# Attention and MLP in one kernel: the first two sets' q and k in two parts, scrap products ahead of the scores, new instruction orders, short MLP stretches as four column tiles

## The chip, the cores and the metric

The kernel runs on one core of one Trainium2 chip. The metric is the device time of one execution in microseconds (us), here the median of three. The profile is one execution recorded by the hardware; its span runs from the first to the last instruction. TensorE (PE) multiplies, VectorE (DVE), ScalarE (ACT) and GpSimd (POOL) do the rest, and SP issues stores. POOL issues nearly all loads[...].

## The reference

```python
B, H, S, Nb, D = 8, 8, 576, 16, 64
k_all = concatenate([beacon_k, k], axis=2)
v_all = concatenate([beacon_v, v], axis=2)
scores = q @ k_all.T / sqrt(D)               # causal over k; every query sees the 16 beacons
a = softmax(scores)
attn = a @ v_all
x = attn.transpose(0, 2, 1, 3).reshape(B * S, H * D)     # 4608 x 512
h = x @ w_in                                  # 512 x 2048
out = (h * sigmoid(1.702 * h)) @ w_out        # 2048 x 512
```

## The kernel before

**Sets.** A set is one batch and four of its eight heads; there are 16 sets. The four heads lie on four groups of 32 partitions. A set's q and k are loaded by POOL (L349) into `qn` and `kn`: each partition takes 18 rows of 64 values. VectorE turns them (`e_turn`, L405) into `qT` and `kT`, with 32 of the 64 head dimensions on partitions and the other two halves side by side; the 16 beacon rows go through `bkf` and `bkn` into the head of `kT`.

**Scores and values.** `e_qk` (L434) computes scores of keys by queries in chunks of up to 512 columns for each of the four heads, as four row tiles of the array (32 rows each) at once. There is one score buffer `s` of four PSUM banks, so chunk i+1 waits until ScalarE has taken the exponential of chunk i (`e_exp`, L445). VectorE (first two sets) or POOL masks the diagonal blocks (L459, L466). `e_av` (L521) multiplies by the values, or by ones for the sums (x = 2), as four column tiles of the array (32 columns each), one head a tile. VectorE makes reciprocals of the sums (`e_z1`, `e_z2`) and scales the values into `xT` (`e_norm`, L556). The first four sets ("early") have their queries cut at `HF` = 288 into half 0 and half 1, and their chunks are cut so that the halves come one after the other; the first two sets' halves 0 come before everything else. Later sets are cut at 224.

**MLP.** Tokens are in groups: 0 and 1 of 256 tokens, then of 512. `e_m1` (L580) computes x @ w_in for a piece of a group, ScalarE (and for groups 0 and 1 VectorE) applies the gate, `e_m2` (L625) multiplies by w_out for groups 0 and 1; from group 2 to 9 a scheme of seven half-size products is used (`e_prod`, L694), with sums on VectorE (L645) and joins (`e_join`, L710). All these use the whole array. The values, m1, m2 and the products share a ring of four PSUM banks `u0` to `u3`; a bank is free again when its closer (gate, norm, evacuation or join) is done.

**Order.** Operations are numbered in the order in which the code creates them. `ORDER` (L16) lists for each engine the numbers in the order in which it executes them; POOL's loads are in POOL's list (Q holds their transfers). `Plan.run` (L146) only merges these lists into one by a model of times and emits the instructions; each engine then runs its own list strictly in order and waits on semaphores. At most eight loads are in flight (`LANES`). By name, TensorE's list begins qk0, qk1, qk2, then value passes of half 0 of sets 0 and 1 (av1.2.0, av0.2.0, av1.0.0, av0.0.0, av1.1.0, av0.1.0), qk3, qk4, m1.0.2, m1.0.0, qk5, m1.0.6, m1.0.4; here av s.x.half is set, x and half, and m1.g.n is group and column block.

Of the kernel before, what the change touches and what calls it, by code (L numbers as in the profile page):

```python
# [8 lines left out]
F32 = mybir.dt.float32  # L9
# [8 lines left out]
        76, 100, 106, 138, 115, 141, 118, 143, 120, 108, 111, 155, 152, 129, 161, 158, 122, 131, 164, 167, 134, 127,  # L18
        170, 173, 176, 145, 125, 148, 150, 177, 182, 188, 191, 227, 194, 197, 232, 183, 203, 234, 200, 178, 237,
        179, 206, 258, 241, 209, 184, 263, 185, 212, 265, 213, 248, 246, 268, 214, 215, 401, 251, 253, 272, 218,  # L20
        404, 275, 244, 279, 219, 220, 407, 282, 284, 277, 221, 414, 320, 296, 304, 290, 302, 292, 300, 298, 312,
        308, 294, 318, 314, 310, 306, 316, 426, 435, 423, 343, 338, 339, 340, 433, 431, 438, 344, 345, 359, 349,
        341, 464, 346, 350, 351, 352, 354, 574, 355, 429, 360, 361, 577, 356, 362, 357, 372, 365, 583, 474, 477,
        373, 366, 374, 367, 605, 480, 484, 375, 482, 607, 368, 506, 502, 488, 492, 610, 490, 486, 498, 504, 500,
        508, 514, 510, 516, 494, 496, 512, 534, 593, 596, 535, 536, 539, 540, 550, 541, 542, 537, 742, 545, 546,
        547, 548, 603, 745, 551, 552, 553, 599, 601, 619, 622, 748, 555, 556, 557, 558, 561, 755, 625, 627, 629,
        562, 563, 776, 568, 564, 569, 570, 571, 779, 764, 767, 659, 637, 641, 657, 649, 651, 647, 661, 635, 631,
        653, 805, 772, 770, 774, 643, 655, 633, 639, 645, 679, 680, 815, 818, 700, 681, 682, 684, 701, 915, 690,
        685, 686, 691, 692, 702, 918, 687, 693, 695, 703, 696, 924, 821, 823, 697, 698, 706, 946, 825, 707, 713,
        708, 709, 948, 934, 937, 714, 715, 716, 827, 951, 944, 940, 942, 853, 831, 833, 855, 857, 851, 843, 835,  # L30
        837, 847, 839, 845, 829, 849, 841, 1083, 960, 963, 875, 876, 880, 877, 878, 881, 882, 1086, 968, 966, 970,
        883, 1089, 902, 909, 903, 886, 891, 1096, 887, 888, 889, 892, 893, 1117, 904, 894, 905, 896, 897, 1120, 898,
        899, 910, 911, 1105, 1108, 1146, 912, 976, 994, 996, 972, 978, 1000, 992, 982, 974, 998, 990, 984, 988, 980,
        1002, 986, 1256, 1156, 1113, 1111, 1115, 1159, 1025, 1020, 1026, 1021, 1259, 1022, 1027, 1031, 1023, 1028,
        1265, 1164, 1162, 1166, 1041, 1042, 1287, 1036, 1047, 1032, 1048, 1033, 1037, 1038, 1034, 1039, 1289, 1054,
        1055, 1049, 1056, 1043, 1044, 1050, 1292, 1057, 1198, 1172, 1168, 1178, 1184, 1180, 1194, 1170, 1174, 1176,
        1275, 1278, 1182, 1186, 1196, 1188, 1190, 1281, 1301, 1285, 1283, 1304, 1216, 1217, 1221, 1192, 1222, 1227,
        1218, 1223, 1228, 1219, 1224, 1232, 1229, 1233, 1230, 1307, 1311, 1309, 1237, 1327, 1333, 1238, 1243, 1234,
        1244, 1235, 1323, 1239, 1245, 1250, 1251, 1341, 1240, 1246, 1252, 1253, 1337, 1405, 1315, 1331, 1343, 1411,
        1335, 1321, 1403, 1431, 1313, 1325, 1407, 1419, 1317, 1423, 1425, 1319, 1339, 1421, 1409, 1329, 1361, 1413,  # L40
        1366, 1382, 1429, 1362, 1363, 1401, 1367, 1364, 1427, 1368, 1383, 1372, 1369, 1373, 1374, 1375, 1388, 1377,
        1389, 1378, 1390, 1395, 1379, 1384, 1380, 1385, 1391, 1396, 1415, 1397, 1398, 1470, 1454, 1417, 1455, 1449,
        1471, 1450, 1451, 1476, 1452, 1456, 1477, 1457, 1478, 1460, 1461, 1462, 1463, 1465, 1466, 1467, 1468, 1472,
        1479, 1473, 1483, 1484, 1485, 1486,
    ],
    "ACT": [
        1, 3, 77, 79, 103, 101, 107, 109, 112, 153, 156, 130, 159, 162, 132, 165, 168, 135, 171, 174, 189, 192, 228,
        195, 198, 233, 235, 201, 204, 238, 180, 207, 259, 210, 264, 186, 266, 269, 216, 402, 405, 408, 222, 417,
        415, 297, 291, 303, 305, 301, 299, 293, 309, 321, 295, 319, 313, 315, 311, 307, 317, 436, 439, 342, 465,
        468, 575, 578, 584, 587, 606, 608, 503, 507, 489, 491, 493, 487, 499, 505, 509, 515, 517, 495, 501, 511,  # L50
        497, 513, 611, 538, 743, 746, 749, 756, 758, 777, 780, 660, 642, 638, 652, 658, 648, 650, 636, 632, 662,
        654, 806, 644, 634, 656, 640, 646, 809, 916, 683, 919, 928, 925, 947, 949, 952, 828, 832, 854, 856, 852,
        858, 834, 838, 844, 840, 836, 846, 830, 848, 850, 842, 1084, 879, 1087, 1090, 1099, 1097, 1118, 1121, 1147,
        1150, 977, 995, 979, 997, 993, 973, 975, 983, 991, 999, 989, 1001, 981, 1003, 985, 987, 1257, 1260, 1024,
        1269, 1266, 1288, 1290, 1293, 1199, 1179, 1173, 1181, 1185, 1195, 1171, 1169, 1175, 1177, 1183, 1187, 1197,
        1189, 1191, 1193, 1220, 1328, 1334, 1324, 1342, 1316, 1332, 1344, 1406, 1412, 1338, 1336, 1404, 1432, 1314,
        1408, 1420, 1318, 1424, 1326, 1426, 1320, 1340, 1422, 1410, 1330, 1322, 1414, 1430, 1402, 1365, 1428, 1416,
        1418, 1453,
    ],
    "DVE": [  # L60
        73, 74, 75, 97, 98, 99, 80, 81, 82, 78, 105, 87, 104, 102, 139, 116, 117, 121, 119, 140, 144, 142, 157, 154,
        123, 163, 160, 124, 224, 169, 128, 166, 172, 175, 146, 147, 126, 149, 151, 225, 226, 398, 190, 193, 196,
        199, 255, 256, 257, 202, 205, 286, 242, 411, 287, 211, 208, 243, 399, 249, 247, 400, 250, 412, 254, 252,
        273, 245, 274, 280, 276, 413, 281, 285, 283, 278, 289, 461, 288, 462, 419, 580, 420, 463, 326, 327, 328,
        421, 322, 92, 323, 324, 422, 427, 428, 424, 425, 325, 330, 334, 329, 335, 432, 336, 331, 434, 337, 332, 333,
        470, 347, 582, 353, 471, 581, 472, 430, 473, 358, 363, 475, 476, 478, 479, 481, 485, 739, 483, 369, 376,
        370, 589, 752, 740, 590, 615, 518, 753, 921, 519, 754, 526, 591, 527, 520, 528, 592, 529, 521, 741, 522,
        597, 523, 594, 530, 595, 598, 531, 802, 532, 524, 533, 616, 543, 525, 604, 549, 617, 618, 554, 600, 620,
        602, 623, 624, 621, 559, 760, 628, 761, 762, 626, 630, 565, 763, 566, 768, 572, 765, 811, 812, 766, 803,
# [47 lines left out]
class Plan:  # L117

    LAT = {"PE": 230, "ACT": 178, "DVE": 212, "POOL": 110, "Q": 1400, "SP": 0}

    def __init__(self, ring):
        self.ops = []
# [71 lines left out]
def kernel(  # L196
# [19 lines left out]
    P = 128  # L216
# [903 lines left out]
```

The softmax here doesn't subtract the row's maximum and nothing guards it: scores larger than these inputs give would overflow.

## Time and profile before

| what | value |
|---|---|
| median of 3 runs | 329.98 us (329.78 to 332.08) |
| span of the profiled execution (the page gives no other time for it) | 328.1 us |
| TensorE busy | 309.3 us, 4288 matmuls |
| first matmul | 8.38 us |
| VectorE, ScalarE, POOL busy | 235.9, 202.0, 114.0 us |
| turning k (128x576), one instruction | 1257 ns |
| first load (k of set 0): issued, landed | 1.30, 5.60 us |
| a w_in load of 256 KB, next landing after the last | about 1.26 us |
| transfers | 28.8 MB; engines nearly full until 57 us |

The times of runs are device times; the span is that of one execution, so a sum of steps is made against the span. In lines of the timeline the first number is the start, the second the length of a group of like instructions up to the end of the last; a matmul's end is modelled and overlaps the next one's start, so distances are taken from start to start. "32*128" is the part of the array in use, rows by columns.

### The profile page before, as it was taken

How to read it: one execution, taken by the hardware profiler on the slowest of the kernel's cores; microseconds unless marked ns; L12 is line 12 of the kernel's file. 1: busy time of each engine (PE TensorE's matmuls, PEld its weight loads, DVE VectorE, ACT ScalarE, POOL GpSimd, SP SyncE). 2: the span in 40 equal slices, each digit the busy share in tenths (PEclk: the TensorE clock that was granted, in tenths of full speed). 3: DMA queues.
4: the chain of work that ended last, by engine and by line, in shares of the span. 5: the costliest groups of instructions: out<-in, count | busy, mean ns of one | idle time of the engine just before them, and what ended most of it. 6: DMA issues, size and time to landing. Idle time of an engine off the chain costs nothing.

```text
span 328.1 us, 9811 instructions
## 1 busy us (share of the span) xinstructions
PE 309.3 (94%) x4288; PEld 210.0 (64%) x4288; DVE 235.9 (72%) x478; ACT 202.0 (62%) x236; POOL 114.0 (35%) x178
## 2 busy tenths in 40 slices
PE   0489999999999999999999999999999999999995
PEld 0367665544775467745878878547764776447884
DVE  3657788777987989977998798958557843006674
ACT  1567597687767686679767686868477212674010
POOL 8765487190319312951078019400042000000000
PEclk9999999999999999999999999999999999999999
DMA  7999999194424921693029809600120012000122
GB/s 126 161 202 209 203 187 181 34 99 103 113 67 72 186 50 34 70 191 57 2 45 177 133 2 122 157 0 2 37 96 2 2 34 78 18 0 2 65 98 97
DMA packets 58219, 28.81 MB, mean 88 GB/s; under 512 B 41280, under 2 KB 53568, under 8 KB 58176
## 3 DMA queue, kind: packets, MB, share of 16 engines
q0 software_dynamic: 47552, 18.49, 47.8%
q1 hardware_dynamic: 10560, 9.69, 9.1%
q8 instruction: 33, 0.54, 0.7%
q14 instruction: 10, 0.08, 0.1%
q10 hardware_dynamic: 64, 0.01, 0.0%
HBM read 37.22 MB, written 9.44 MB: 142 GB/s over the span
## 4 chain that ended last, share of the span: by engine, by line
PE 89%; ACT 4%; DVE 3%; DMA 2%; issue 1%; POOL 0%; DVEq 0%; ACTq 0%; POOLq 0%
PE u L580 36%; PE u L694 30%; PE s L434 9%; PE u L521 9%; PE u L625 4%; ACT E L445 3%; DMA qn<-in_q_dram 2%; DVE qT L405 1%; DVE sA L645 1%; DVE xT L556 1%; DVE rz L544 0%; DVE zt L533 0%; ACT L601 0%; DVE osb L710 0%; DVE rc L540 0%
## 5 line engine op out<-in xcount | busy, mean ns | idle before, releaser
L580 PE MATMUL u<-xT,w 128*128 128x512 f16 (+1 forms) x704 | 130.4, 340 | 0.5 <-ACT g L601 0.5
L445 ACT ACTIVATE E<-s 128x2048 f16<-128x2048 f32 (+5 forms) x66 | 98.9, 1515 | 46.0 <-PE s L434 45.6
L601 ACT ACTIVATE g<-u 128x512 f16<-128x512 f32 x128 | 70.5, 598 | 53.8 <-PE u L580 53.4
L580 PEld LDWEIGHTS <-w 128*128 128x128 f16 x704 | 67.8, 98 | 53.9 <-issue 1.5
L466 POOL TENSOR_SCALAR_AFFINE_SELECT E<-E 128x512 f16<-128x512 f16 (+3 forms) x78 | 49.3, 663 | 113.4 <-ACT E L445 81.6
L710 DVE SCALAR_TENSOR_TENSOR osb<-u,osb 128x512 f32<-128x512 f32 x56 | 37.2, 682 | 24.7 <-PE u L694 22.4
L694 PEld LDWEIGHTS <-g 128*128 128x128 f16 x512 | 48.4, 98 | 9.3 <-issue 0.2
L694 PE MATMUL u<-w,g 128*128 128x256 f16 x384 | 50.6, 273 | 0.0
L434 PE MATMUL s<-qT,kT 32*128 32x32 f16 (+20 forms) x1376 | 35.4, 232 | 14.4 <-DVE qT L405 8.4
L434 PEld LDWEIGHTS <-kT 32*128 32x128 f16 x1376 | 25.8, 94 | 30.6 <-issue 15.0
L694 PEld LDWEIGHTS <-sA 128*128 128x128 f16 x384 | 36.3, 98 | 5.3 <-issue 0.3
L694 PE MATMUL u<-tB,sA 128*128 128x256 f16 x256 | 35.0, 273 | 0.1
L645 DVE TENSOR_TENSOR sA<-g 128x512 f16<-128x512 f16 x32 | 12.9, 415 | 26.2 <-ACT g L601 26.2
L556 DVE TENSOR_TENSOR xT<-u,rz 128x352 f16<-128x352 f32 (+2 forms) x52 | 25.6, 517 | 6.9 <-PE u L521 6.7
L365 POOL DMA_DIRECT2D vb<-in_v_dram x32 | 27.4, 874 | 2.3 <-DMA kn<-in_k_dram 1.5
L521 PE MATMUL u<-E,vb 128*32 128x352 f16 (+8 forms) x928 | 28.0, 267 | 0.0
L484 DVE TENSOR_TENSOR zs<-zs,E 128x1344 f16<-128x1344 f16 (+2 forms) x36 | 22.7, 633 | 5.3 <-POOL E L466 4.4
L521 PEld LDWEIGHTS <-vb 128*32 128x32 f16 (+1 forms) x928 | 20.2, 99 | 5.9 <-issue 1.7
L405 DVE STREAM_TRANSPOSE kT<-kn 128x576 f32<-128x576 f32 x16 | 20.1, 1258 | 2.4 <-DMA kn<-in_k_dram 1.6
L405 DVE STREAM_TRANSPOSE qT<-qn 128x576 f32<-128x576 f32 x16 | 19.8, 1239 | 0.1
L533 DVE STREAM_TRANSPOSE zt<-u 128x224 f32<-128x224 f32 (+2 forms) x32 | 14.9, 471 | 6.6 <-PE u L521 6.5
L484 DVE TENSOR_TENSOR zs<-E 128x1856 f16<-128x1856 f16 x12 | 15.8, 1319 | 3.3 <-POOL E L466 3.3
(44 smaller groups left out, 237.7 us busy)
## 6 DMA issues: line engine op xcount, KB each, us to landing
out_dram<-osb SPq DMA_DIRECT2D x36, 256.0 KB, 2.5
kn<-in_k_dram POOLq DMA_DIRECT2D x16, 288.0 KB, 6.7
qn<-in_q_dram POOLq DMA_DIRECT2D x16, 288.0 KB, 6.6
vb<-in_v_dram POOLq DMA_DIRECT2D x24, 128.0 KB, 6.6
w<-in_moe_w_in_dram POOLq DMA_DIRECT2D x8, 256.0 KB, 9.9
w<-in_moe_w_out_dram POOLq DMA_DIRECT2D x4, 512.0 KB, 14.2
vb<-in_v_dram POOLq DMA_DIRECT2D x8, 112.0 KB, 5.0
vb<-in_v_dram POOLq DMA_DIRECT2D x8, 80.0 KB, 7.9
```

Of the source, the lines that this page charges most:

```text
L365: nc.gpsimd.dma_start(out=t[0 : hi - lo, j, h0:h1, :], in_=v[b, h0:h1, lo:hi, :].rearrange("h n d -> n h d"),)
L405: nc.vector.transpose(out=f32(dst.rearrange("p n e -> p (n e)")).rearrange("p (r t) -> p t r", t=TR), in_=f32(src[:, :]).rearrange("p (t c ...
L434: nc.tensor.matmul(sc[:, h, o : o + w], kT[s % NB2][r : r + 32, j * P : (j + 1) * P, d], qT[s % NB2][r : r + 32, a : a + w, d], start=(d = ...
L445: nc.scalar.activation(out=Es[s][:, :, c0:c1], in_=ss[i][:, :, o : o + c1 - c0], func=AFT.Exp, scale=0.125,)
L466: nc.gpsimd.affine_select(out=blk, in_=blk, compare_op=ALU.is_ge, fill=0.0, base=off + (Nb if j == 0 else 0), pattern=[[0, Q], [1, w]], ch ...
L484: nc.vector.tensor_tensor(out=t, in0=E[:, :, Z0:S] if i == 1 else t, in1=E[:, :, wcol[i] : wcol[i] + S - a], op=ALU.add,)
L521: nc.tensor.matmul(u[32 * h : 32 * h + 32, a:e], lhs, src[0:kw, h, col : col + e - a], start=first, stop=last,)
L556: nc.vector.tensor_tensor(out=xT[:, 2 * hs + x : 2 * hs + x + n, t0 : t0 + w], in0=rings[("av", s, x, half)][:, 0 : n * w].rearrange("p (n ...
L580: nc.tensor.matmul(u[:, o + a - t0 : o + e - t0], w1t[:, kp, nt * P : (nt + 1) * P], xT[:, kp, a % XR : (e - 1) % XR + 1], start=(kp == 0) ...
L601: nc.scalar.activation(out=gts[g][:, n0:n1, 0:w], in_=rings[("m1", g, n0)][:, 0 : n * w].rearrange("p (n w) -> p n w", n=n), func=AFT.Gelu ...
L694: nc.tensor.matmul(u[:, HM * mt : HM * (mt + 1)], lhs[:, n, mt * P : (mt + 1) * P], rhs[:, n, :], start=(n == 0 and mt == 0), stop=(n == H ...
L710: nc.vector.scalar_tensor_tensor(out=osbs[(g, dst)][:, :], in0=rings[("p", g, p)][:, :], scalar=scale_of(g), in1=osbs[(g, src)][:, :], op0 ...
```

## The change

1. `HF` becomes 256, so that half 0 of the early sets is group 0 of the MLP. Half 0 of a set has 416 score columns instead of 512; the three other chunks have 416 instead of 384.
2. The first two sets' q and k are loaded and turned in two parts, rows 0 to 255 and rows 256 to 575. The tail of `kT` that isn't yet there is set to zero at the start. The second part is turned after the set's first score chunk, which still reads zeros there. All q and k loads are written with heads and rows as two dimensions. POOL's list now begins: k part 1 of set 1, k, q of set 0, q of set 1 (all part 1), v block 0, beacon v, k rest of set 0, two w_in loads, q rest of set 0, v blocks 1 and 2, keep, two w_in loads, q and k rest of set 1.
3. Scrap products in fp32 of a tile filled with 1.7 and -0.6, 512 and 384 columns wide before qk0 and 256 before qk1, go into bank u3.
4. In half 0 of the early sets too the two value passes x = 0 and 1 share one bank and one norm.
5. Operations of the MLP from group 2 on that stand in a short stretch (20 matmuls or fewer) next to values are emitted as four column tiles: each matmul becomes four, of 32 weight columns each, into the same bank.
6. All five order lists are new, and stores order the joins that reuse their buffers in the planner. TensorE's list begins qk0, qk1, qk2, av0.2.0, av0.0.0, av1.2.0, av1.0.0, qk3, qk4, m1.0.2, m1.0.0, qk5, m1.0.6, av0.2.1, qk6, m1.0.4, qk7, m1.0.8, m1.0.10, qk8. VectorE's begins with the casts of both beacons, k and q of set 0, k and q of set 1 (part 1), a memset, k rest, a mask, q rest of set 0, five masks, then z1, z2, z1, a memset, z2, two norms, and the rest of set 1; then a gate, z1, k of set 2, z2, a gate, q of set 2, three gates.

```diff
-    LAT = {"PE": 230, "ACT": 178, "DVE": 212, "POOL": 110, "Q": 1400, "SP": 0}
+    LAT = {"PE": 230, "ACT": 178, "DVE": 212, "POOL": 110, "Q": 1400, "SP": 2200}
+    def tiled(self):
+        runs, late = [], False
+        for i in ORDER["PE"]:
+            o = self.ops[i]
+            late = late or o.name.startswith("m1.2.")
+            if not runs or runs[-1][0] != o.mode:
+                runs.append([o.mode, [], late])
+            runs[-1][1].append(o)
+        got = set()
+        for x, y, z in zip(runs, runs[1:], runs[2:]):
+            if y[0] == "m" and y[2] and "c" in (x[0], z[0]) and sum(o.count for o in y[1]) <= 20:
+                got.update(o.seq for o in y[1])
+        return got
...
-                        if o.mode != mode:
-                            dur += 95 + 0.75 * tail / 2.4
-                        mode, tail = o.mode, o.tail
+                        m = "c" if o.seq in small else o.mode
+                        if m != mode:
+                            dur += 114
+                        mode = m
...
-    HF = S // 2
+    HF = 256
...
-    nc.vector.memset(bkf[:, 0:1, :], 0.0)
-    nc.vector.memset(bkf[:, 1:HS, :], 0.0)
+    nc.vector.memset(bkf[:, 0:HS, :], 0.0)
+    scrap = sA[0][:, 0:4, :].rearrange("p a n -> p (a n)").bitcast(F32)
+    for i, x in enumerate((1.7, -0.6)):
+        nc.vector.memset(scrap[:, i::2], x)
+    nc.vector.memset(ones, 1.0)
     for t in kT:
-        nc.vector.memset(t[:, NK:, :], 0.0)
-    nc.vector.memset(ones, 1.0)
+        nc.vector.memset(t[:, Nb + HF :, :], 0.0)
+    FILL = {"qk0": (512, 384), "qk1": (256,)}
...
-    def rows_of(t, s):
+    ENDS = ((0, S), (0, HF), (HF, S))
+
+    def e_load_qk(s, which, part):
         b, hs = divmod(s, HS)
-        return t[b, Q * hs : Q * hs + Q].rearrange("h (r t) d -> (h r) (t d)", t=TR)
-
-    def e_load_qk(s, which):
+        a, e = ENDS[part]
         dst = (qn, kn)[which][s % NB3]
-        nc.gpsimd.dma_start(out=dst[:, :], in_=rows_of((q, k)[which], s))
+        nc.gpsimd.dma_start(
+            out=dst[:, a // 32 * D : e // 32 * D],
+            in_=(q, k)[which][b, Q * hs : Q * hs + Q, a:e].rearrange("h (r t) d -> h r (t d)", r=32),
+        )
...
+    def mm(o, lhs, rhs, start, stop):
+        if not tiled[0]:
+            nc.tensor.matmul(o, lhs, rhs, start=start, stop=stop)
+            return
+        for r in range(0, P, 32):
+            nc.tensor.matmul(o[r : r + 32], lhs[:, r : r + 32], rhs, start=start, stop=stop)
...
+        turned(s, 1 if s < HS else 0, [qks[i] for i in CH_OF.get(s - NB2, [])])
+
+    def turned(s, part, deps):
+        a, e = ENDS[part]
         for which in (1, 0):
-            deps = [ld_qk[(s, which)], cast if which else None]
-            turn[(s, which)] = op(
-                "DVE", 1090 + 245 * which, deps + [qks[i] for i in CH_OF.get(s - NB2, [])],
-                lambda which=which: e_turn(s, which),
-                pr=0 if urgent else 4, due=max(0, due_of(s) - 12000), name=f"turn{s}",
+            turn[(s, which, part > 1)] = op(
+                "DVE", 40 + 1050 * (e - a) / S + 245 * (which and a == 0),
+                deps + [ld_qk[(s, which, part > 1)], bkc[s] if which else None],
+                lambda which=which: e_turn(s, which, part), name=f"turn{s}.{part}",
             )
...
+        if CHUNKS[i][0][0] < HS and CHUNKS[i][0][1] == 0:
+            turned(CHUNKS[i][0][0], 2, [qks[i]])
...
-        order = [(2, 1), (2, 0), (0, 0), (0, 1), (1, 1)] if whole else [
-            (x, h) for h in range(2) for x in (2, 0, 1)
-        ]
+        order = [(2, 1), (2, 0), (0, 0), (0, 1), (1, 1)] if whole else [(2, 0), (0, 0), (2, 1), (0, 1), (1, 1)]
...
-    load_bk(0, 1, (), ("SP", "ACT"))
-    load_bk(1, HS)
-    load_qk(0, 1)
-    load_qk(0, 0)
-    load_qk(1, 1)
-    load_qk(1, 0)
+    load_bk(0, HS, (), ("SP", "ACT"))
+    for s in range(HS):
+        load_qk(s, 1, part=1)
+        load_qk(s, 0, part=1)
...
     w1_cols(0, 512)
+    for s in range(HS):
+        load_qk(s, 1, part=2)
+        load_qk(s, 0, part=2)
...
+    small = plan.tiled()
+    idle = psu.tile([P, 512], F32, tag="u3", name="u3")
     for o in order:
+        for w in FILL.get(o.name, ()):
+            nc.tensor.matmul(idle[:, 0:w], scrap[:, 0:P], scrap[:, 0:w], start=True, stop=True)
+        tiled[0] = o.seq in small
         o.emit()
```

`e_m1`, `e_m2` and `e_prod` call `mm` in place of the matmul.

## The prediction

> **What bounds the kernel now.** I read the page first, then the busy time by stretch, then TensorE's timeline.
>
> ```profile
> PE 309.3 (94%) x4288; PEld 210.0 (64%) x4288; DVE 235.9 (72%) x478; ACT 202.0 (62%) x236; POOL 114.0 (35%) x178
> ...
> PE   0489999999999999999999999999999999999995
> ...
> DMA  7999999194424921693029809600120012000122
> ...
> PE 89%; ACT 4%; DVE 3%; DMA 2%; issue 1%; POOL 0%; DVEq 0%; ACTq 0%; POOLq 0%
> ```
>
> TensorE carries 89% of the chain that ended last and leaves idle time only in the first two slices and the last. The stretches say how much:
>
> ```profile
> 0.00:20.49 20.49, 6.45 (x200) 5.34 (x201) 12.14 (x31) 8.06 (x7) 15.66 (x30) 1.00 1.25 154
> 20.49:324.27 303.78, 302.82 (x4100) 204.70 (x4088) 223.07 (x446) 193.94 (x229) 98.29 (x150) 1.00 0.53 82
> 324.27:328.10 3.83, 0.00 (x0) 0.00 (x0) 0.69 (x1) 0.00 (x0) 0.00 (x0) 1.00 0.60 205
> ```
>
> The first number after a stretch is its length, the second TensorE's busy time: 14 us idle up to 20.49, then 303.78 us without a break, then a tail of 3.83 (one join, one store). So only three things count: when the unbroken work begins, how long it is, and the tail. The start, TensorE then VectorE:
>
> ```profile
> 8.38 1.04 PE L434 MATMUL s<-qT,kT 32*128 32x288 f16 x24 [8.38 <-DVE qT L405]
> 11.47 1.04 PE L434 MATMUL s<-qT,kT 32*128 32x288 f16 x24 [2.04 <-ACT E L445]
> 14.54 0.83 PE L434 MATMUL s<-qT,kT 32*128 32x288 f16 x24 [2.04 <-ACT E L445]
> 15.30 1.05 PE L521 MATMUL u<-E,ones 128*32 128x288 f16 x24
> ...
> 20.49 1.92 PE L580 MATMUL u<-xT,w 128*128 128x256 f16 x16
> ```
> ```profile
> 5.70 1.26 DVE L405 STREAM_TRANSPOSE kT<-kn 128x576 f32<-128x576 f32 x1 [1.62 <-DMA kn<-in_k_dram]
> 7.07 1.26 DVE L405 STREAM_TRANSPOSE qT<-qn 128x576 f32<-128x576 f32 x1
> ```
>
> The first score chunk waits for whole k and q, each 1.26 us to turn; each later chunk waits for the exponential before it. The same 24 matmuls take 1.04 us here and about 0.54 from 17.9 on.
>
> Inside the unbroken work the cost to look for stands between stretches of different array shape: r (32 rows, scores), c (32 columns, values), m (whole array, MLP).
>
> ```profile
> 47.41 0.41 PE L521 MATMUL u<-E,ones 128*32 128x288 f16 x12
> 47.75 1.05 PE L580 MATMUL u<-xT,w 128*128 128x256 f16 x8
> ...
> 49.59 0.54 PE L434 MATMUL s<-qT,kT 32*128 32x288 f16 x24
> 50.06 1.90 PE L625 MATMUL u<-w,g 128*128 128x512 f16 x8
> ```
> ```profile
> 224.61 1.92 PE L694 MATMUL u<-w,g 128*128 128x256 f16 x16
> 226.47 0.65 PE L434 MATMUL s<-qT,kT 32*128 32x272 f16 x24
> ...
> 233.02 0.61 PE L694 MATMUL u<-w,g 128*128 128x256 f16 x4
> ...
> 237.05 0.65 PE L434 MATMUL s<-qT,kT 32*128 32x400 f16 x24
> ```
>
> Read from start to start. An m stretch of 16 takes 1.86 us and one of 36 (233.02 to 237.05) 4.03, so a matmul of 256 columns costs 0.109 and leaving the stretch about 0.11. The c stretch at 47.41 takes 0.34 us; its 512 columns, four tiles at once, need 0.213 and its twelve matmuls 0.010, so leaving costs 0.114. The r stretch at 49.59 takes 0.47; 768 columns need 0.320, 24 matmuls 0.025, leaving 0.126. A line through all stretches gives leaving m 0.106 plus 2.5 ns a matmul, r 0.126 plus 1.0 ns, c 0.114 plus 0.8 ns. What those don't explain is 1.9 us of waits in eight places (0.65 of it in the first whole m1 block at 66.3).
>
> [...] The trace agrees: 0.11 to 0.13 us at all 144 changes. [...] value groups of four tiles, each with its weight load, follow each other in 40 ns at 80 columns and 150 at 352, width/2.4 plus 3 ns or more[...]. [...] The trace agrees: its clock record rises at 17.7, after 3.2 us of work. [...]
>
> **The change, part by part.**
>
> *Column tiles.* Numbering the operations as the code creates them, the old PE list has 145 stretches, as the trace has: 52 changes out of r, 35 out of c, 57 out of m. The new list, its 153 short MLP operations counted as c, has 108: 52, 29 and 26. Changes cost 52x0.126 + 35x0.114 + 57x0.106 = 16.6 us now, 52x0.126 + 29x0.114 + 26x0.106 = 12.6 then: -4.0. Without the tiles the new list would change 200 times and cost 6.1 us more than now (52 of r, 59 of c, 89 of m), so all depends on the tiles. The 153 operations hold 612 matmuls, each now four; a group costs 4x0.8 = 3.2 ns over its columns against 2.5: +0.5. Sum **-3.5**. Not shown: four tiles that stream the *same* columns. Lower bound 0 extra (value groups)[...]. I take 0: in the value groups loads and streams overlap at every width. Quadrupled matmuls add nothing on other engines: each operation still ends in one signal.
>
> *Start.* A part is 256 of 576 rows, so turning k or q takes 0.56 instead of 1.26. Before, k0 landed at 5.60 and whole loads followed 1.45 apart, thus 0.65 for a part. The new POOL order is k1, k0, q0, q1 (parts), v block 0, beacon v, k0 rest, two w1, q0 rest, v blocks 1 and 2, keep, w1 again, then the rest of set 1. Two cases:
> - All 16 engines: 4.17 (5.60 less one whole load) plus parts: k0 at 5.45, q0 at 6.1; turned 6.7; qk0 6.7. Then q0 rest behind v 0.75 + 0.17, k0 rest 0.8, w1 2x1.3, itself 0.8: 12.0; qk2 needs it turned, 12.75. VectorE's queue holds masks and the chain z1, z2, z1, a 0.49 memset, z2, two norms behind that turn: masks 1.2, then 0.43+0.65+0.43+0.49+0.65+0.69+0.69 = 4.0: the first m1 at 18.1 instead of 20.49.
> - Four engines: the source of a part steps over 4 heads outermost[...]. From the w1 packets (1 KB each 80 ns per engine) a part takes 2.6: k0 lands near 6.6, q0 7.1, qk0 7.8; q0 rest, 3.2 on its four engines, 13.5, qk2 14.25, v block 2 about 15.2, first m1 19.3.
> I take the second[...]: -1.2 at the first m1. But half 0 shrinks from 288 to 256 tokens, so six value passes of 96 columns (0.24) and 96 score columns (0.08) move behind that point: +0.3. Start **-0.9**, bounds -2.4 and +1.0 (a part late by 2 us). Four more loads issue on POOL, 4x0.57 = 2.3, ahead of its first masks; POOL waits for exponentials 81.6 us in all, so they hide, and masks are what they would delay. The second set's beacon loads now share SP and ScalarE's queue ahead of the table load (0.45 an issue), done before 3.5; exponentials start after 8.
>
> *Scrap products.* 512, 384 and 256 columns in fp32, before qk0 and qk1. [...] If they raise the clock early, qk0 and qk1 save 0.5 each and four value passes 1.0, but qk2 waits for q0 rest and the first m1 for VectorE: worth 0 to -0.4 there; I take 0. Their two memsets (0.27 each, as the bkf memset of 256) and larger kT memsets put about 1.3 us on VectorE before k lands at 5 or later: hidden.
>
> *Double norms, first four sets.* Two norms of 256 become one of 512: four instructions fewer on VectorE, hidden under TensorE: 0.
>
> *New orders.* ScalarE keeps its 13 table switches; VectorE 223 and ScalarE 194 of 303.8 stay below TensorE. Behind the first m1, VectorE reaches turn k2 and q2 with three gates queued behind; by the load order k2 lands near 22, q2 near 24.6; a late one holds the gates, the four PSUM banks and TensorE. The 1.9 us of old waits can close, or others open: bounds -1.9 and +2.5. The planner's flat 114 ns a change and 3.2 a value group equal what I measured, where the old formula was up to 20 ns off, so I take a third closed: **-0.6**. Store waits in the join order move nothing: output buffers are the same four.
>
> *Tail.* Product 5 ends four matmul pairs, 1.3 us, ahead of the last; its two joins (0.68 each) plus latency push the last join by **+0.1**.
>
> Sum: -3.5 - 0.9 - 0.6 + 0.1 = -4.9; 328.1 becomes 323.2. The runs' median is 1.9 above the profiled span, so **325.1**.
>
> **Rivals.**
> - *Loads starve set 2 (0.16).* If whole q and k loads, now written as heads by rows too, also run on four engines, 1.43 becomes 5.8: q2 lands near 29 instead of 24.6, gates queue behind its turn, TensorE idles about 3.5, and the start gain goes (0.9): 325.1 + 4.4 = 329.5. [...] Against: the whole set is contiguous, so its dimensions can merge.
> - *Waits return (0.12).* 37 fewer changes but VectorE or ScalarE late in tight stretches, +3.5: 328.6. For: exponentials pace TensorE at the start, one score buffer. Against: 80 us of VectorE slack.
> - *Tiles aren't free (0.07), the slower side.* Four tiles reading the same moving columns, or weight loads showing[...]. The gain is gone from 8 ns a group (4.9/0.612), slower by 1% from 13. Against: the 40 ns value groups.
> - *The start doesn't move* (inside the forecast's upper end): 326.0.
>
> **How the numbers follow.** The forecast has 0.65, its own range 322 to 327: low end with 16 engines and more waits closed. Measured beside no change, about 1% can be told: faster means below 326.7, slower above 333.3. Faster 0.60 of the forecast, 0.06 of the first two rivals, 0.04 of cases better still: 0.70. Same 0.05, 0.16 from the first two rivals: 0.21. Slower 0.07 of the tiles and 0.02 of starving: 0.09. The range takes the forecast and most of the first two rivals: 321.5 to 329.5.
>
> **What would show it.** Right: 108 stretches, about 1.86 us for a tiled stretch of 16 at 256 columns, starts of groups 110 ns apart; qk0 near 7.8 and the first m1 near 19.3; scrap wholly before qk0; unbroken work about 300. Wrong: groups over 117 ns apart; qk0 after 8.4; TensorE waiting on VectorE's qT turn between 20 and 30; qk0 at half clock as before.

## The result and the profile after

The changed kernel takes 338.82 us (median of 6 runs, 337.52 to 341.21) against 330.50 for the kernel before in the same series: ratio 1.0254, 95% interval 1.0219 to 1.0289. The profiled execution spans 336.9 us against 328.1: 8.8 us more. It is slower, where 325.1 was forecast.

From the page of the kernel after: the engines' busy time, the queue that carries instructions, and the shares of the chain that ended last.

```profile
PE 313.6 (93%) x6274; PEld 221.4 (66%) x6274; DVE 237.2 (70%) x479; ACT 200.8 (60%) x236; POOL 119.6 (36%) x182
...
q8 instruction: 49, 0.80, 1.0%
...
PE 78%; DVE 8%; DMA 6%; ACT 4%; issue 3%; POOL 0%; DVEq 0%; ACTq 0%; POOLq 0%
```

TensorE is still the engine that counts, but its share of the chain fell from 89% to 78%. Its matmuls rose from 4,288 to 6,274, and a queue that the prediction never looked at now brings 49 packets of 16 KB, where the page of before has 33:

```profile
q8 instruction: 33, 0.54, 0.7%
```

The busy time by stretch, cut where the prediction cut it, then in parts (after each stretch: length, busy time of TensorE, its weight loads, VectorE, ScalarE, POOL; granted clock, DMA share, GB/s; where the clock record has nothing yet, as ahead of 21.2 us here, the view prints 1.00):

```profile
0.00:24.10 24.10, 10.42 (x207) 6.76 (x207) 11.14 (x34) 7.63 (x7) 16.07 (x29) 1.00 1.11 126
24.10:332.79 308.69, 303.21 (x6079) 214.65 (x6068) 225.36 (x445) 193.16 (x229) 103.53 (x154) 0.99 0.55 83
332.79:336.90 4.11, 0.00 (x0) 0.00 (x0) 0.71 (x2) 0.00 (x0) 0.00 (x0) 0.80 0.37 128
```
```profile
24.10:60.00 35.90, 34.62 (x601) 24.18 (x591) 23.01 (x40) 27.12 (x30) 24.21 (x40) 0.95 1.31 182
60.00:250.00 190.00, 185.90 (x4527) 133.84 (x4528) 160.62 (x316) 134.28 (x148) 77.67 (x111) 1.00 0.59 81
```

The work after the start was forecast at about 300 us without a break; it takes 308.7, and over 4 us of it are idle between 60 and 250, where TensorE of before was idle for 0.7. The sum of what happened: the first MLP matmul begins 3.6 later (24.10 for 20.49), the work after it takes 4.9 more (308.7 for 303.8), the tail 0.3 more.

The 4.9 split up, with the prices of the prediction (which hold: the tiled stretch at 201.42 has 84 matmuls and takes 2.43 us, 2.26 for its columns, 0.07 for its matmuls, 0.11 for leaving it): changes of shape -4.0, tiles +0.5, work moved out of the start +0.3, and what these prices leave over, 1.9 before and 10.0 after: **+8.1**. It is called waits here, though some 1.6 of the 10.0 are matmuls at half the clock. The waits of after lie at: 24 to 33 us, 2.4; 34.9, 0.65; 65.8, 0.4; 93.7, 1.5; 130.9 to 132.6, 1.5; 138.5 to 145, 0.8; 184.2, 1.5; 207, 0.2; 219 to 250, 1.1. From 34.9 us on nearly all are inside stretches of column tiles (those of the values counted) or just ahead of them.

**The start.** TensorE's timeline of the kernel after, then VectorE's:

```profile
1.67 3.35 PE L1137 MATMUL u<-sA 128*128 128x512 f32 x4 [1.67 <-DVE sA L280]
10.88 0.89 PE L458 MATMUL s<-qT,kT 32*128 32x256 f16 x24 [5.86 <-DVE kT L422]
...
18.29 0.88 PE L458 MATMUL s<-qT,kT 32*128 32x320 f16 x24 [3.87 <-DVE E L483]
...
24.10 3.11 PE L598 MATMUL u<-xT,w 128*128 128x256 f16 x16
```
```profile
9.21 0.64 DVE L429 STREAM_TRANSPOSE kT<-kn 128x256 f32<-128x256 f32 x1 [5.11 <-DMA kn<-in_k_dram]
...
17.39 0.74 DVE L429 STREAM_TRANSPOSE qT<-qn 128x320 f32<-128x320 f32 x1 [3.06 <-DMA qn<-in_q_dram]
```

A part is turned in half the time, as forecast (0.64 for 1.26), but parts land far later: k of set 0 at 9.12 (whole before: 5.60), its q at 10.17 (7.05), the rest of that q at 17.37. The wait ahead of 18.29 is named after a mask; what TensorE waited for is the rest of q, turned at 18.1. The sixteen first MLP matmuls take 3.11 us, not 1.92: the clock record grants half the clock from 24.6 to 28.1 us, in the stretch whose mean is 0.95.

**A wait inside a stretch.** Two places on TensorE's timeline of after:

```profile
95.82 0.62 PE L601 MATMUL u<-tB,sA 128*32 128x256 f16 x15
97.09 0.28 PE L601 MATMUL u<-tB,sA 128*32 128x256 f16 x1 [0.65 <-issue]
...
189.81 2.58 PE L601 MATMUL u<-xT,w 128*32 128x256 f16 x86
193.30 1.38 PE L601 MATMUL u<-xT,w 128*32 128x256 f16 x42 [0.91 <-issue]
```

At 97.09 the last of sixteen tile matmuls stops though the fifteen ahead of it, on the same operands, ran: no engine and no data can be late there, and the profile names none ("issue").

### The profile page after: what moved, and what is told of

Same layout as the page of the kernel before. It is cut to its first block, busy times and chain, and to the rows that moved or that the text cites. A ratio compares the mean times of both kernels' runs of the same rounds, so it can differ in the third digit from the quotient of the medians.

```text
span 336.9 us, 13766 instructions
## 1 busy us (share of the span) xinstructions
PE 313.6 (93%) x6274; PEld 221.4 (66%) x6274; DVE 237.2 (70%) x479; ACT 200.8 (60%) x236; POOL 119.6 (36%) x182
## 2 busy tenths in 40 slices
DMA packets 61819, 29.09 MB, mean 86 GB/s; under 512 B 44352, under 2 KB 57664, under 8 KB 61760
## 4 chain that ended last, share of the span: by engine, by line
PE 78%; DVE 8%; DMA 6%; ACT 4%; issue 3%; POOL 0%; DVEq 0%; ACTq 0%; POOLq 0%
PE u L598 40%; PE u L601 22%; PE u L546 8%; PE s L458 8%; DMA kn<-in_k_dram 4%; ACT E L469 3%; DMA qn<-in_q_dram 2%; DVE sA L679 1%; DVE osb L744 1%; ACT g L635 1%; DVE zs L508 1%; DVE zt L558 1%; ACT L635 1%; DVE kT L429 1%; DVE rz L569 1%
## 5 line engine op out<-in xcount | busy, mean ns | idle before, releaser
L469 ACT ACTIVATE E<-s 128x2048 f16<-128x2048 f32 (+4 forms) x66 | 98.9, 1515 | 55.6 <-PE s L458 54.1
L598 PE MATMUL u<-xT,w 128*128 128x512 f16 (+1 forms) x456 | 87.2, 346 | 0.0
L601 PE MATMUL u<-xT,w 128*32 128x512 f16 (+1 forms) x992 | 47.0, 338 | 1.1 <-issue 0.9
L458 PE MATMUL s<-qT,kT 32*128 32x32 f16 (+17 forms) x1376 | 35.6, 233 | 13.3 <-DVE kT L422 5.9
L598 PE MATMUL u<-w,g 128*128 128x256 f16 (+1 forms) x232 | 37.9, 302 | 0.0
L598 PEld LDWEIGHTS <-g 128*128 128x128 f16 x324 | 30.9, 98 | 10.3
L601 PEld LDWEIGHTS <-w 128*32 128x32 f16 x992 | 27.1, 96 | 14.1 <-issue 1.9
L546 PE MATMUL u<-E,vb 128*32 128x352 f16 (+9 forms) x928 | 31.1, 266 | 1.0 <-DVE osb L744 0.4
L581 DVE TENSOR_TENSOR xT<-u,rz 128x352 f16<-128x352 f32 (+3 forms) x48 | 25.5, 546 | 7.2 <-PE u L546 6.9
L601 PE MATMUL u<-w,g 128*32 128x256 f16 x864 | 29.7, 273 | 0.0
L601 PEld LDWEIGHTS <-g 128*32 128x32 f16 x1008 | 25.9, 97 | 1.7 <-issue 0.3
```

Source lines behind the costliest of these rows:

```text
L458: nc.tensor.matmul(sc[:, h, o : o + w], kT[s % NB2][r : r + 32, j * P : (j + 1) * P, d], qT[s % NB2][r : r + 32, a : a + w, d], start=(d = ...
L469: nc.scalar.activation(out=Es[s][:, :, c0:c1], in_=ss[i][:, :, o : o + c1 - c0], func=AFT.Exp, scale=0.125,)
L546: nc.tensor.matmul(u[32 * h : 32 * h + 32, a:e], lhs, src[0:kw, h, col : col + e - a], start=first, stop=last,)
L581: nc.vector.tensor_tensor(out=xT[:, 2 * hs + x : 2 * hs + x + n, t0 : t0 + w], in0=rings[("av", s, x, half)][:, 0 : n * w].rearrange("p (n ...
L598: nc.tensor.matmul(o, lhs, rhs, start=start, stop=stop)
L601: nc.tensor.matmul(o[r : r + 32], lhs[:, r : r + 32], rhs, start=start, stop=stop)
```

## The experiments

### First theories: parts on few DMA engines, tiles, VectorE

**1. Parts in 128 pieces.** Each part is read as 128 equal pieces instead of four heads (the rows come in another order). That more engines then share it is an estimate.

```diff
-            in_=(q, k)[which][b, Q * hs : Q * hs + Q, a:e].rearrange("h (r t) d -> h r (t d)", r=32),
+            in_=(q, k)[which][b, Q * hs : Q * hs + Q].rearrange("h (r t) d -> (h r) (t d)", t=TR)[:, a // 32 * D : e // 32 * D],
```

> The changed kernel, but a part of q and k is read as 128 equal pieces (8 or 10 rows out of each 18), so that its outermost dimension is 128 instead of 4 heads; same bytes, packets of the same size, same order; the tokens are permuted, so the output is another one. Theory (four engines per part load delay the start): a part lands in about 0.7 us, k of set 0 near 5.5 instead of 9.1, the first m1 near 18 instead of 24.1, the time 338.8 - 5 to -6, near 333. Rival (the start is late because of the scrap products or the order of VectorE): the loads land earlier but the first m1 stays after 22, time above 337.

337.21 us, ratio 1.0186 (1.0134 to 1.0237). k of set 0 lands at 5.04, its q at 6.99, the rest of that q at 14.45; VectorE's and TensorE's timelines:

```profile
5.13 0.64 DVE L429 STREAM_TRANSPOSE kT<-kn 128x256 f32<-128x256 f32 x1 [0.41 <-DMA kn<-in_k_dram]
```
```profile
7.70 0.90 PE L458 MATMUL s<-qT,kT 32*128 32x256 f16 x24 [2.68 <-DVE kT L422]
...
21.82 3.38 PE L598 MATMUL u<-xT,w 128*128 128x256 f16 x16
```

The shape of the transfer alone is worth 4.1 us at the landing of k and 2.3 at the first MLP matmul. The rest of the delay stays, the slow first MLP matmuls included (3.38 us for the sixteen, 1.92 in before). The trace doesn't name a transfer's engines, but from 2.5 to 6.5 us the DMA share is 0.52 in after and 1.05 here (47 and 134 GB/s), as fewer engines for a part would have it. One thing more differs: for the same data the page of after counts 44,352 packets under 512 B and that of this run 41,280; what these 3,072 cost no run separates.

**2. Whole loads for the first two sets**, and whole turns; k and q of set 0 are loaded ahead of k of set 1, and only `kT` behind its last key is set to zero. All else is as after.

```diff
     def e_load_qk(s, which, part):
...
+        if part == 2:
+            return
+        part = 0
...
```

> The changed kernel with whole loads and whole turns for the first two sets too (k, q of set 0, then of set 1; the second parts are left out), everything else kept. Theory (part loads delay the start): qk0 near 8.4, the first m1 near 20, the time near 338.8 - 4 = 335. Rival (the loss is in the new orders alone): the time stays within 1 us of 338.8.

338.05 us, ratio 1.0209 (1.0128 to 1.0291). First MLP matmul at 21.26, again at half clock (3.59 us for the sixteen); the waits from there on, half clock included, are 11.8 us (10.0 in after). Even without the split the start is 0.8 later than before's, and the loss behind it is whole: it is not an echo of the start.

**3. No tiles, and tiles alone.** After with the short stretches left in mode m; and the kernel before with the tiling rule only (53 operations, 216 matmuls in the trace, 20 changes fewer).

```diff
-        tiled[0] = o.seq in small
+        tiled[0] = False
```

> The changed kernel without column tiles: short MLP stretches use the whole array. Theory (tiles work as computed: 92 changes of mode at 0.11 each are saved): up to 10 us slower than the changed kernel, less where TensorE waits anyway, so 343 to 348. Rival (tiles are what slows the kernel: weight loads or four tiles streaming the same columns): 330 to 338, faster than the changed kernel.

> The kernel before with the column tiles alone (same rule; its own order has 53 such operations and 20 fewer changes of mode). Theory: 20 x 0.114 = 2.3 us saved, 0.2 paid for more matmuls, so about 2 us faster than before, 328.4. Rival (tiles cost time): not faster than before, above 330.

Without tiles: 343.89 us, ratio 1.0382 (1.0327 to 1.0436), 197 changes in the trace from the first MLP matmul on, and the waits fall from 10.0 to 4.8 us. About 1.5 of these 5.2 are the clock, not the tiles: in the profiled execution of this run it is full from 21.7 us on, and the sixteen first MLP matmuls take 1.92 us, after the same scrap products. By the prices 93 changes less 0.5 should have made 9.6 us between the two; the runs have 5.1. The tiles alone, on before: 330.70, ratio 0.9986 (0.9962 to 1.0011): most of the 2 us that 20 changes cost is given back in waits, 3.4 for 1.9. So column tiles save what they were forecast to save, and waits come with them: some 3.7 us in after.

**4. VectorE's load.** The 128 sums of half products on VectorE replaced by copies of their first operand (the result of the second MLP product is then another), in after, in before, and in before with tiles. A copy of 512 columns takes 0.29 us, a sum 0.43.

```diff
-            add(eng, s1, a21, a22, ALU.add)
+            nc.vector.tensor_copy(out=s1, in_=a21)
...
```

> The changed kernel with each of the 128 sums of the product scheme replaced by a copy of its first operand (the second is left out, the output is another one), which should about halve 54 us of VectorE's work. Theory A (after the start, TensorE waits because VectorE is late in the new order): the 6 us of waits between 60 and 250 mostly go, time near 332 to 334. Theory B (it waits for ScalarE's exponentials or for loads): waits stay, time within 1.5 of 338.8.

> The kernel before with the same copies. TensorE has 1.9 us of waits in all, so at most 1 us faster than before, 329.5 to 330.5, under both theories; a larger gain would mean that VectorE sets the pace of the kernel before as well.

> The kernel before with column tiles and with the copies. Theory A (tiles save their 2 us, but VectorE's lateness eats it): 2 us faster than the kernel before with copies, near 328. Theory B (ScalarE's exponentials pace TensorE there): no faster than the kernel before with copies.

After: 339.22, ratio 1.0236 (1.0172 to 1.0300), waits 10.8 us, though VectorE is busy for 149.5 of the 190 us from 60 to 250, not 160.6. Before: 330.19, ratio 0.9991 (0.9974 to 1.0008). With tiles: 328.98, ratio 0.9963 (0.9943 to 0.9983), waits 2.3. For the few tiles of before, a lighter VectorE does return 1.2 of the 2 us. For after it returns nothing, though one wait named after VectorE, at 131 us, shrinks from 1.13 to 0.43. That a late VectorE makes most of the waits is not borne out; but the copies saved a third of the sums' time (53 to 36 us), not the half expected, so the test is not a strong one.

### Scrap and the clock

**5. Scrap without gaps, on before**: 512 four times and 384 columns ahead of qk0, 512 and 384 ahead of qk1 and qk2.

> The kernel before with scrap products alone, but enough to keep TensorE busy from 1.7 to about 8 and between the first score chunks (512, 512, 512, 512, 384 columns before qk0, 512 and 384 before qk1 and qk2). Theory [...]: full clock from about 5, score chunks 0.55 instead of 1.07, value passes 1.3 instead of 2.6, first m1 near 18 instead of 20.5, the time 2 us below before, 328.4. Rival (fp32 products of a scrap tile don't raise the clock): first m1 and time unchanged or later by the last scrap product.

331.24, ratio 0.9999 (0.9974 to 1.0024). The clock is full from 5.1 us on, 3.4 us after the scrap began; the first two score chunks take 0.64 instead of 1.04, the first MLP matmul starts at 18.95 instead of 20.49; then the fifth waits, on "issue", until 20.91, and most of the gain is gone.

```profile
18.95 0.63 PE L583 MATMUL u<-xT,w 128*128 128x256 f16 x4
20.91 1.47 PE L583 MATMUL u<-xT,w 128*128 128x256 f16 x12 [1.33 <-issue]
```

This profiled execution is one of four whose mean clock is 1.000, at 329.7 to 330.0 us. In the other eight it is 0.989 to 0.995 and the time 331.0 to 332.4, so scrap without gaps does not always hold the clock.

**6. The same in kernel 1** (after with parts in 128 pieces; ahead of qk2 four products of 512 columns and one of 384), and **7. weights first**: the scrap of 5 on before, with the third and fourth MLP weight load issued ahead of the last two value loads of set 0.

```diff
-        8, 10, 12, 14, 16, 17, 19, 21, 23, 25, 27, 29, 31, 33, 35,
+        8, 10, 12, 14, 16, 17, 19, 21, 23, 25, 27, 33, 35, 29, 31,
```

> The kernel after with its part loads in 128 equal pieces, as in the earlier run, and with scrap that goes on: four products of 512 and one of 384 columns ahead of qk0 and of qk2, 512 and 384 ahead of qk1. The earlier run took 337.2 us and its first sixteen MLP matmuls 3.38 us at half the clock from 21.82. If the scrap of the change ends too early and that is what loses the clock: full clock from 5.1 us on, the MLP matmuls from about 21.2 in 2.2 us, 2 us gained, 335.2. If the scrap delays the scores, or the clock falls between qk2 and the MLP all the same: 337 or more.

> The kernel before with scrap products ahead of qk0 (four of 512 columns, one of 384), qk1 and qk2 (512 and 384 each), and with the third and fourth loads of the first MLP weights issued ahead of set 0's last two value loads. In the run with that scrap alone the fifth MLP matmul waited from 19.55 to 20.91 us, and the fourth weight load landed at 20.84. If that load is what held it: it lands near 18.5, the MLP matmuls go on from 18.95 without the wait, and 1.0 to 1.5 us are gained: 329.0 us, ratio 0.996. If VectorE's second half of xT held it, or if the loads behind take the gain back: 330.5, ratio 1.000.

6 takes 341.20, ratio 1.0329 (1.0301 to 1.0358): the clock is full from 5.3 to 22.3 us, yet the last two matmuls of qk4 wait 0.99 on "issue", the MLP starts at 21.81 and is caught by half clock from 22.3 to 25.7 (3.14 us for the sixteen), and another wait of 2.2 us ends at 37.25. 7 takes 330.99, ratio 1.0002 (0.9977 to 1.0026), and its timeline of TensorE refutes what I expected:

```profile
19.29 0.62 PE L583 MATMUL u<-xT,w 128*128 128x256 f16 x4
20.89 2.72 PE L583 MATMUL u<-xT,w 128*128 128x256 f16 x12 [0.97 <-issue]
```

The fourth weight load landed at 19.20, and the fifth matmul still began at 20.89. That load did not hold it. (The twelve take 2.72 us because the clock record has half clock from 20.0 to 26.8 us in this execution.)

### Second theory: TensorE's own instructions

In the trace the waits on "issue" of after, of 5, 6 and 7 have two things in common. They stand at matmul 223, 479, 1,502, 2,653, 3,805, ... in TensorE's order: 221 plus a multiple of 128, give or take two. And in each case a packet of 16 KB of the instruction queue had ended 1.2 to 1.7 us earlier. The page of after counts 6,274 weight loads beside 6,274 matmuls, so 128 pairs are 256 instructions; 6,274 pairs make 49 such lots, the 49 packets of the page, as 4,288 pairs make 33 and the page of before has 33. I take a packet for one block of 256 instructions, with a border behind it. The traces fit a single block ahead: over all traces here a block's packet starts at most 1.6 us after TensorE passes into the block before it if no load is under way, and if loads fill the DMA engines 0.7 to 3.6 us after in eight of ten cases, 5.9 at most. What a border costs, 8, 9, 10 and 12 measure.

**8. Tiles alone at the end.** Before, and after its last matmul 512 tile matmuls each of 64, 128 and 256 columns.

```diff
+    for n in (64, 128, 256):
+        for i in range(128):
+            for r in range(0, P, 32):
+                nc.tensor.matmul(spare[r : r + 32, 0:n], keep[:, r : r + 32], w1t[:, 0, 0:n], start=True, stop=True)
```

> The kernel before, and after its last matmul 1,536 more column-tile matmuls that nothing waits for and that wait for nothing: 512 of 64 columns, 512 of 128, 512 of 256. Theory supply (TensorE's instructions arrive in blocks of 256, a load of weights and a matmul each, and a block takes some 3.4 us to have): each 512 takes no less than about 13.8 us, 27 ns a matmul, whatever its columns, the first some 4 us less: 38 us in all. Rival pipeline (a tile matmul costs its columns at a quarter of 2.4 a ns and 0.8 ns more): 3.8, 7.2 and 14.1 us, 25 in all.

370.32 us (one run). TensorE's timeline:

```profile
323.93 1.45 PE L1095 MATMUL u<-w,keep 128*32 128x64 f16 x155
328.18 1.90 PE L1095 MATMUL u<-w,keep 128*32 128x64 f16 x128 [2.80 <-issue]
331.63 1.90 PE L1095 MATMUL u<-w,keep 128*32 128x64 f16 x128 [1.56 <-issue]
...
356.91 3.68 PE L1095 MATMUL u<-w,keep 128*32 128x256 f16 x128 [0.33 <-issue]
```

The first 155, what was in hand, start 8 ns apart; from then on every 128 start 3.45 us apart (twice 3.73) whether they are 64 or 128 columns wide: 27 ns a pair. At 256 columns, which stream in 3.5, they start 4.0 apart (352.90, 356.91, 360.91). The trace has the same three pieces in each: the packet starts 1.1 us after the border, moves for 1.0 to 1.4 us, and 1.4 us later TensorE goes on; the 3.73 and the 4.0 are the longer packets. The clock is half from 327.9 to 341.5 us and full after that, and 3.45 stands in both, so it is not the pace of the array. The three groups take 12.5, 14.2 and 16.8 us (start to start), not 3.8, 7.2 and 14.1: the supply theory, and at 256 columns a little beyond it.

**9. Each tile matmul in two halves**, in after.

```diff
-            nc.tensor.matmul(o[r : r + 32], lhs[:, r : r + 32], rhs, start=start, stop=stop)
+            h = rhs.shape[-1] // 2
+            for a in (0, h):
+                nc.tensor.matmul(o[r : r + 32, a : a + h], lhs[:, r : r + 32], rhs[:, a : a + h], start=start and a == 0, stop=stop and a == h)
```

> The kernel after with each column-tile matmul of the MLP cut into two of half its columns: the same columns, the same changes of mode, 2,448 more pairs of a weight load and a matmul. Rival pipeline: 0.8 ns more for each, 2 us, 341 us, and waits as before this cut. Theory supply: stretches of 256 columns fall from 27 to 13 ns a matmul and so are held at some 27 ns: at least 10 us more, up to 40: 350 to 380 us, with the waits inside the column-tile stretches.

395.32 us (one run), beyond the upper end. The page's instruction queue and TensorE's waits:

```profile
q8 instruction: 69, 1.13, 1.2%
```
```profile
PE u L603 <- issue: 34.0, 25, 3.1
PE u L546 <- issue: 6.8, 6, 2.8
```

The page of after has 49 packets here. The columns and the changes of shape are the same, 2,640 pairs are added, and it takes 56.5 us more than the kernel after. TensorE waits 46 us on "issue" (these two and 5.3 at score matmuls), each time within two matmuls of a border; in after 2.5.

**10. The border moved.** Kernel 7 with 158 tile matmuls of 64 columns while TensorE waits anyway (those ahead of qk1 in place of a scrap product of 384 columns), so that the border falls ahead of qk2.

```diff
...
+    PAIRS = {"qk1": 150, "qk2": 8}
...
```

> The last start run (the kernel before, scrap, weights first) with 158 column-tile matmuls of 64 columns added while TensorE waits anyway: 150 ahead of qk1 in place of the scrap product of 384, 8 ahead of qk2. There the fifth MLP matmul waited 0.97 us, 1.25 us after a block of instructions had arrived, and the blocks' seam lay at that matmul. Theory supply: with 156 more pairs ahead of it the seam falls just ahead of qk2, where TensorE waits for ScalarE anyway, and the next at the start of qk4; the MLP matmuls go on without a wait from about 19.3, and 0.6 to 1.3 us are gained against that run: 329.6 us, ratio 0.997. Rival, a load or VectorE holds the fifth MLP matmul: it waits until 20.9 as there, 331 us, ratio 1.000 or more.

334.84, ratio 1.0128 (1.0102 to 1.0155): the time was mispredicted, since the wait at the new place is three times as long and the MLP, now from 24.45 us, runs at half clock (3.05 us for the sixteen). The place was right to within a matmul.

```profile
14.29 0.28 PE L437 MATMUL s<-qT,kT 32*128 32x288 f16 x1 [0.18 <-ACT E L448]
17.46 0.82 PE L437 MATMUL s<-qT,kT 32*128 32x288 f16 x23 [2.90 <-issue]
```

qk2's second matmul is number 224. TensorE entered the block before at 10.3, but the packet of the next began to move at 15.1, 4.8 us later, with the DMA engines full of loads (in kernel 5 the same block began 3.7 us after its border). The matmul goes on 1.4 us after the packet's end. The wait at the fifth MLP matmul is gone. As the MLP starts 5 us later here, that alone doesn't clear loads and VectorE; that the wait went where the border went is what speaks against them.

**11. Only wide tiles**: column tiles for stretches of the first MLP product alone (512 columns).

```diff
-            if y[0] == "m" and y[2] and "c" in (x[0], z[0]) and sum(o.count for o in y[1]) <= 20:
+            if y[0] == "m" and y[2] and "c" in (x[0], z[0]) and sum(o.count for o in y[1]) <= 20 and all(o.dur > 150 * o.count for o in y[1]):
```

> The kernel after with column tiles for the first MLP product's stretches only (512 columns a matmul, 188 matmuls in 17 stretches), not for the second's 256 columns (46 stretches): 168 changes of mode by the lists, against 107 with all and 200 with none. Theory supply: a tile of 512 columns streams 53 ns, twice what a block's supply allows, so no wait at seams is added; 32 changes at 0.115 us less 0.5 us for the tiles, 3.2 us below the run with none: 340.7 us, 0.10 us a change; all tiles gave 5.1 us for 93 changes, 0.055 each. Rival, tiles bring waits of VectorE and ScalarE forward whatever their columns: about 0.055 us a change, 342.1 us.

343.08, ratio 1.0368 (1.0319 to 1.0417): the rival's value, even above it. One wait of 1.1 us at a border remains (until 195.55), so saving only the wide tiles doesn't make a kernel safe. In the profiled executions the first sixteen MLP matmuls take 2.97 us here and 1.92 in 3; this and the wait make up some 2.1 of the 2.4 us by which the forecast of the theory was missed. So this run decides nothing between the two.

**12. Without later loads**: q, k, v and beacon values of the third to eighth batch are not loaded, in after and in before; those batches compute on the data of the first two.

```diff
...
+        if b > 1:
+            return
...
```

> The kernel after without the loads of q, k, v and of the beacon values for the third to eighth batch: those batches compute on what the first two left in the buffers. In the kernel after four waits of TensorE at the seams of its instruction blocks, at 37.5, 96.2, 143.3 and 192.1 us, come to 3.1 us; each of those blocks began to move 1.6 to 2.2 us after the seam at which the one before it was begun, while loads filled the DMA engines, and blocks asked for with no load under way began 0 to 1.1 us after it. Theory supply behind loads: the three waits after 90 us go, 2.4 us, and the smaller ones with them: 335.5 us, less if loads held other things. Rival, the blocks are late by TensorE's pace alone: the three stay, 338 us.

> The kernel before without the same loads, as the measure of what those loads cost where no wait stands at a seam: its waits are 1.9 us in all after the first MLP matmul. Both theories: 329 to 330.5 us.

After: 336.98, ratio to the kernel before 1.0184 (1.0143 to 1.0226), 1.8 us less than after (the two intervals just overlap). Before: 330.90, ratio 1.0014 (0.9986 to 1.0041), nothing. The place at 189.81 of after is now one group on TensorE's timeline, all 128 of it without a wait:

```profile
189.96 3.68 PE L605 MATMUL u<-xT,w 128*32 128x256 f16 x128
```

All three border waits after 90 us are gone (stretches at 93.7, 141.7 and 184.2: 3.6 us of waits in after, 1.0 now), and a small one of 0.14 opens at 198.95, where 128 pairs were run in 3.4 us. Waits after 60 us fall from 6.9 to 4.0; those ahead of 60 us, where the loads that stay are under way, rise by 1.6 in this execution (the sixteen first MLP matmuls take 3.59 us, and the border wait of 37.5 is 1.28, at 40.1), so less is gained than the 3.3 us forecast. So after 60 us loads in the DMA engines and the pace of the tiles make these waits together: there either alone costs nearly nothing with these lists.

## Why the prediction failed

Of the 13.7 us between the forecast of 325.1 and the 338.8 measured, 8.7 lie in the waits, 4.8 in the start and 0.2 in the tail; the changes and the tiles themselves are as forecast.

- **"Quadrupled matmuls add nothing on other engines: each operation still ends in one signal."** The step that failed first. They add nothing on other engines, but each is two instructions on TensorE (6,274 weight loads for 6,274 matmuls), and once it had used up what was in hand, blocks of 256 came every 3.45 us at best in 8. Without the later loads 2.9 of the 6.9 us of waits after 60 us go, nearly all at borders (12). The 0.65 at 37.5 stands at a border too, but without tiles it stays (0.86 in 3), so the tiles are not its cause.
- **Tiles -3.5.** Sizes right: changes cost what was forecast, groups of four tiles of 256 columns start 109 ns apart (110 forecast), and the rival of dear tiles did not come. Its extra 8 ns a group, the point of decision that it named, is nearly reached if the borders are counted: the trace has 660 groups (6,274 matmuls less 4,294 without tiles, by three; the forecast counted 612), and 4.5 us are missing between the run without tiles and after: 7 ns a group, or some 5 if the clock's 1.5 is taken off. All tiles together gain 5.1 us with these lists, but the lists without tiles stand at 343.9.
- **Old waits -0.6**, bounds -1.9 to +2.5: measured +8.1, outside both. About 3.5 are borders. About 1.6 are the half clock in the first MLP matmuls. Some 0.8 stand ahead of a score chunk at 31 us in all kernels with the new lists. The rest, some 2 us, are new waits in single places: 1.1 of them at 131 us, where TensorE's view of waits names VectorE's join. The second rival ("waits return", +3.5) was right in kind and short in size; VectorE as its cause holds for a part only.
- **Start -0.9**: measured +3.9 (3.6 at the first MLP matmul and the 0.3 of moved work), outside +1.0. The case I took was right in kind: parts do suffer from their four-headed source, and 1 undoes it (k of set 0 at 5.04 for 9.12, the small packets named there left aside). That four engines carry a part was my estimate, which no trace shows, and the size was off: the four parts land at 6.89, 9.12, 10.17 and 11.04, where I let k0 land at 6.6 and q0 at 7.1; why they take so long no run shows further. The rest of q came at 17.37, not 13.5.
- **Scrap 0.** Its own time ahead of the scores is 3.35 us, all hidden. What it does to the clock stays open, as no run leaves it out of after: it ends at 5.0, TensorE then idles for 5.9 us, and in the clock record after is full only from 21.2 to 24.6 and at half again until 28.1, under the first MLP matmuls, while 3, with the same scrap, is full there. Before was full from 17.7 on. Scrap that goes on keeps the clock in 4 of the 12 executions of 5, and there the earlier scores only bring the first border forward.
- **Norms 0, tail +0.1**: the tail grew by 0.3; the norms show nowhere.
- **First rival, loads starve set 2**: the loss is not there (whole loads of k take 5.7 us to land in the median, 6.7 before); but the same loads do hold up TensorE's blocks (2.9 us of waits after 60 us go without the later ones, 12).

What stays open: the remaining 2 us of small waits after 60 us, in single places; when the clock falls to half under the first MLP matmuls, which differs between executions of like starts; and whether tiles pay with lists made with the borders in view, which was not tried. No kernel here beats the kernel before by more than its interval except before with tiles and copies, which leaves work out.

## What to carry to other kernels

Count TensorE's instructions as a resource of its own: a matmul is two (6,274 weight loads for 6,274 matmuls in after), and in 8 a stretch of small tiles got a pair every 27 ns at best once what was in hand was used up; under loads the block at 37.5 us of after came later still. Cutting a product into tiles to save changes of shape cost waits here where 128 pairs lasted less than the next block took to come: 3.45 to 4.0 us in 8 with no load under way, some 4.8 at the border at 37.5 us of after, under loads. Their mark is a wait without any releaser that comes back at multiples of 128 matmuls. When a split load lands must be measured before its half-size is worth anything (the first part of k at 9.12 us in after and 5.04 in 1, the whole k of before at 5.60). A warm-up that ended 5.9 us ahead of the real work was not to be counted on (half clock from 24.6 to 28.1 us in after, full from 21.7 in 3), nor one that went on (4 of 12 executions of 5 kept the clock).

## What the hardware showed beyond that

- Where TensorE waited for a block of 256 instructions in these traces, the block's packet moved for 0.9 to 1.9 us, and TensorE went on 1.2 to 1.7 us after it; the packet started up to 1.6 us after the last border with quiet DMA engines, up to 5.9 with busy ones.
- Tile pairs of 64 columns started 8 ns apart while instructions lasted (the first 155 in 8).
- The later loads, for which TensorE does not wait at 97, 143 and 193 us of after, cost it 0.5 to 1.1 us each time there, through the instruction queue (12).
